# Rebuilding phi's derivative from the stored features instead of storing it: an interleaved linear-attention and sliding-window kernel, forward and backward

## The chip, the cores and the metric

The kernel runs on one core of a Trainium2 chip. The metric is the time of one execution in device microseconds; before the change the median of 3 runs is 2331.71 us (2330.03 to 2334.66). The profile shown is one further execution.

## The reference

Four layers run in turn on x of shape 2048 x 640 (32 heads of width 20), each as `x = x + block(layernorm(x))`: linear attention (A), sliding-window attention (B), A, B. The outputs are the final x and the gradients of A_x and of the four weight matrices (A's and B's are used twice each, so their gradients are summed over two layers). What matters here is block A:

```
phi = lambda t: jnp.where(t > 0, t + 1, jnp.exp(t)) + 1e-6
pq, pk = phi(q), phi(k)
kv = jnp.einsum("bhsd,bhse->bhde", pk, v)
z = jnp.einsum("bhsd->bhd", pk)
num = jnp.einsum("bhqd,bhde->bhqe", pq, kv)
den = jnp.einsum("bhqd,bhd->bhq", pq, z)[..., None] + 1e-6
o = num / den
```

The derivative of phi is min(exp(t), 1). It is also min(phi(t) - 1e-6, 1), since phi is at least 1 wherever t is positive.

## The kernel before

The 2048 rows are 16 tiles of 128 rows; a row's 640 features are handled in two chunks of 320. The run has these parts, one after the other (times from the trace):

- Forward. First the q, k, v projection of layer 0 for all tiles (to about 118 us), then passes in which layer 0's output, layer 1's window attention and layer 2's projection are interleaved by tile, then layer 3's (to about 780 us). `a_qkv` makes pq and pk: ScalarE writes `e = exp(t)` (L456), VectorE cuts it to min(e, 1) (L457) and adds max(t, 1e-6) to it (L460). Per tile SP stores pq (160 KB), e for q and k together (320 KB) and kv, that is pk beside v (320 KB), for the backward.
- Backward. `bwd_phase` and `B_attn_bwd` take turns. The linear-attention layers 2 and 0 are done in the two later calls of `bwd_phase` ("wide"). Each wide call first runs `tail` for the layer above and `lin_dO`; then `lin_grads` makes dq, dk and dv of the linear layer, tile by tile, together with `tail` of the same layer and, in the call for layer 2 only, `turn_g` and `local_dO` for the layer below. These two stretches are called the **first gradient stage** (layer 2, about 1388 to 1511 us) and the **last gradient stage** (layer 0, about 2164 to 2266 us).

Inside `forward` and `bwd_phase` nothing is ordered by hand: each operation is given to `Sched` with an engine, an assumed duration and the buffers it reads and writes. `Sched` lays all of them out with its assumed durations, lowest priority number first among those that are ready, and emits each engine's instructions in the order so found. On the chip every engine then goes through its own fixed order, and an instruction whose input is late holds everything behind it on that engine. SP issues most DMAs, among them the DMA transposes ("flips").

Names used below, per tile of a gradient stage, with the line and the engine:

- `q0 q1 k0 k1`: VectorE multiplies a chunk of dphi(q) or dphi(k) in PSUM by the derivative, `ee`, into dqkv (L1184). v0, v1 are copied by ScalarE (L1180).
- the flip `dqT<-dqkv` (L837, SP) turns the q and k part of dqkv once k1 is written; a TensorE turn and a VectorE copy (L866) do the rest. They feed 30 matmuls with wq (L843).
- `dh`: ScalarE takes the two chunks of their result (L991). Then VectorE forms three sums (L999 to L1005, the last called `sm`), ScalarE `w` (L1006), GpSimd `gw` (L1009, 128x640 f32), VectorE `gcar` (L1011), which is the running gradient.
- only in the first gradient stage: a turn of gcar with the copy `gT` (L866), matmuls with WoB, two VectorE evacuations `slab a` and `slab b` (L1052), GpSimd `prod` (L1059), VectorE `dd` (L1062) and two small operations (L1064, L1066), and the store `dOpt<-slab`, issued by ScalarE.
- loads per tile on SP: dNT and kvT (flips), `ee` (320 KB, ring of 2 buffers), hn (160 KB), and in the first gradient stage o.

In the steady part of the first gradient stage VectorE's order is gcar, q0, dd with its two small ones, q1, gT, L999 to L1005, dqT copy, k0, slab a, k1, slab b, and again gcar. ScalarE's is dh of chunk 0, the store of dOpt, dh of chunk 1, w, v0, v1. GpSimd alternates gw and prod. In the last gradient stage VectorE's order is gcar, q0, q1, L999 to L1005, dqT copy, k0, k1.

Of the kernel before, what the change touches and what calls it, by code (L numbers as in the profile page):

```python
# [11 lines left out]
ALU = mybir.AluOpType  # L12
AX = mybir.AxisListType
BF = mybir.dt.bfloat16
F32 = mybir.dt.float32
I32 = mybir.dt.int32
P = 128
# [15 lines left out]
def dve_ns(n):  # L33
    return 150 + 1.04 * n
# [139 lines left out]
class Kern:  # L174
    def __init__(self, ctx, tc, x0, A_wqkv, A_wo, B_wqkv, B_wo, grad_out, outs):
# [5 lines left out]
        D, T = self.D, self.T  # L181
# [62 lines left out]
        self.sv = {}  # L244
        for l in (0, 2):
            self.sv[l] = dict(
                pq=d.tile([T, D], BF, name=f"pq{l}"), e=d.tile([T, 2 * D], BF, name=f"e{l}"),
                kv=d.tile([T, 2 * D], BF, name=f"kv{l}"), o=d.tile([T, D], BF, name=f"o{l}"),
                r32=d.tile([T, self.H], F32, name=f"r32{l}"),
                mbd=d.tile([D, D + P], BF, name=f"mbd{l}"),  # L250
            )
# [53 lines left out]
    def forward(self):  # L305
# [7 lines left out]
        with ExitStack() as st:  # L313
# [44 lines left out]
            def dma(eng, out, in_, size, r, w):  # L358
                def f():
                    with nc.allow_non_contiguous_dma(reason="strided layouts"):  # L360
                        dq[eng].dma_start(out=out(), in_=in_())
                op(eng, 60, f, r, w, dma=("D", size))
# [71 lines left out]
            def a_qkv(l, tt, hnT):  # L434
                sv = self.sv[l]
                e, p_ = R["ee"].buf(), R["pp"].buf()

                def chunk(ci):
                    def f():
                        c0 = ci * CW  # L440
                        ps = R["half" if l == 0 and ci in (0, 2) else "mm"].buf()
                        mm_chunk(ps, CW, [(lambda k=k: hnT.t[:, k, :], lambda k=k: wsb["Wqkv_A"][:, k, c0:c0 + CW],
                                           k == 0, k == DT - 1) for k in range(DT)], [hnT, ("Wqkv_A", ci)])
                        if ci >= 4:
                            o = c0 - 2 * D
                            if ci == 4:
                                op("ACT", av(CW), lambda: nc.scalar.copy(vv[:, tt, o:o + CW], ps.t[:, 0:CW]), [ps],
                                   [("vv", tt, ci)])
                            else:
                                op("DVE", vp(CW), lambda: nc.vector.tensor_copy(vv[:, tt, o:o + CW], ps.t[:, 0:CW]),  # L450
                                   [ps], [("vv", tt, ci)])
                                dma("SP", lambda: self.tm_view(sv["kv"])[:, tt, :], lambda: kv[:, tt, :], 320 * KB,
                                    [("pk", tt, 2), ("pk", tt, 3), ("vv", tt, 4), ("vv", tt, 5)], [])
                            return
                        es = lambda: e.t[:, c0:c0 + CW]
                        op("ACT", av(CW), lambda: nc.scalar.activation(es(), ps.t[:, 0:CW], ACT.Exp), [ps], [(e, ci)])  # L456
                        op("DVE", v4(CW), lambda: nc.vector.tensor_scalar(  # L457
                            out=es(), in0=es(), scalar1=1.0, scalar2=None, op0=ALU.min), [], [(e, ci)])
                        pd = (lambda: p_.t[:, c0:c0 + CW]) if ci < 2 else (lambda: pk[:, tt, c0 - D:c0 - D + CW])
                        op("DVE", vp(CW), lambda: nc.vector.scalar_tensor_tensor(  # L460
                            out=pd(), in0=ps.t[:, 0:CW], scalar=1e-6, in1=es(), op0=ALU.max,
                            op1=ALU.add), [ps, (e, ci)], [(p_, ci) if ci < 2 else ("pk", tt, ci)])
                        if ci == 3 and l == 0 or ci == 1 and l != 0:
                            turn("half" if l == 0 else None, lambda: pqT[:, :, tt * P:(tt + 1) * P], lambda: p_.t[:, 0:D], DT,
                                 [(p_, 0), (p_, 1)], [("pqT", tt)])
                            dma("SP", lambda: self.tm_view(sv["pq"])[:, tt, :], lambda: p_.t[:, 0:D], 160 * KB,
                                [(p_, 0), (p_, 1)], [])
                        if ci == 3:
                            dma("SP", lambda: self.tm_view(sv["e"])[:, tt, :], lambda: e.t, 320 * KB,
                                [(e, i) for i in range(4)], [])  # L470
                    return f
                return [chunk(ci) for ci in range(6)]

# [328 lines left out]
    def bwd_phase(self, lb, la, nb, ahead=()):  # L802
# [8 lines left out]
        with ExitStack() as st:  # L811
# [18 lines left out]
            def dma(eng, out, in_, size, r, w):  # L830
                def f():
                    with nc.allow_non_contiguous_dma(reason="strided layouts"):
                        dq[eng].dma_start(out=out(), in_=in_())
                op(eng, 60, f, r, w, dma=("D", size))
# [59 lines left out]
            if wide:  # L894
                for name, n, shape, dt in (
                        ("dh", 1, [P, D], F32), ("w", 1, [P, D], F32), ("gw", 1, [P, D], F32), ("sm", 3, [P, 8], F32),
                        ("scr", 1, [P, D], BF), ("pq", 2, [P, D], BF), ("dNT", 2, [P, DT + 1, P], BF),
                        ("kvT", 2, [P, 2 * DT, P], BF), ("ee", 2, [P, 2 * D], BF)):
                    R[name] = ring(name, n, shape, dt)
            if not wide:  # L900
                R["om"] = ring("om", 2, [P, TT, P])
# [14 lines left out]
            def load(name, src, tt):  # L916
                b = R[name].buf()
                dma("SP", lambda: b.t, lambda: self.tm_view(src)[:, tt, :], 256 * src.shape[-1], [], [b])
                return b
# [227 lines left out]
            def lin_grads(tt, items, t0):  # L1147
                c = {}
                sv = self.sv[la]
                row = slice(tt * P, (tt + 1) * P)  # L1150

                def start():
                    for nm, src, size in (("dNT", self.tmp_dN, 192 * KB), ("kvT", sv["kv"], 320 * KB)):
                        c[nm] = b = R[nm].buf()
                        flip(lambda b=b: b.t, lambda src=src: src[row, :], size,
                             [("dNd", tt)] if nm == "dNT" else [], [b])
                    c["ee"] = load("ee", sv["e"], tt)

                def chunk(kind, ci):
                    def f():  # L1160
                        ps = R["mm"].buf()
                        e0 = ci * CW
                        ks = [k for k in range(DT) if not (self.band[k][1] <= e0 or self.band[k][0] >= e0 + CW)]
                        src, k0, rhs, key, col = {"q": ("dNT", 0, mbdT, "mbdT", 0), "k": ("kvT", DT, dmbdT, "dmbdT", D),
                                                  "v": ("kvT", 0, dmbd, "dmbd", 2 * D)}[kind]
                        b = c[src]

                        def right(k, x0, x1):
                            return lambda: rhs[:, k, e0 + x0:e0 + x1]
                        mm = [((lambda k=k: b.t[:, k0 + k, :]), right(k, x0, x1), x0, x1)  # L1170
                              for k in ks for x0, x1 in [(max(self.band[k][0] - e0, 0), min(self.band[k][1] - e0, CW))]]
                        if kind == "v":
                            mm[0] = (mm[0][0], right(ks[0], 0, CW), 0, CW)
                        else:
                            mm = [((lambda: onesx) if kind == "k" else (lambda: b.t[:, DT, :]), right(DT, 0, CW), 0, CW)] + mm
                        keys = ["mbdT"] if kind == "q" else [(key, m) for m in range(DT)]
                        banded(ps, mm, [b] + keys)
                        dst = lambda: dqkv[:, tt, col + e0:col + e0 + CW]
                        if kind == "v":
                            op("ACT", act_ns(CW), lambda: nc.scalar.copy(dst(), ps.t[:, 0:CW]), [ps],  # L1180
                               [("dqkv", tt, "v")])
                        else:
                            e, x0 = c["ee"], (D if kind == "k" else 0) + e0
                            op("DVE", dve_ns(CW), lambda: nc.vector.tensor_mul(dst(), ps.t[:, 0:CW], e.t[:, x0:x0 + CW]),  # L1184
                               [ps, e], [("dqkv", tt, kind)])
                    return f
                items.append((t0 - 0.6, start))
                for i, (kind, ci) in enumerate((k, ci) for k in "qkv" for ci in range(2)):
                    items.append((t0 + 0.15 * i, chunk(kind, ci)))
# [337 lines left out]
```

## Time and profile before

| what | value |
|---|---|
| median of 3 runs | 2331.71 us |
| the profiled execution | 2343.73 us, its span 2342.0 us, mean granted clock 0.953 |
| TensorE busy | 2051.8 us, 88% of the span |
| VectorE busy | 1470.7 us, 63% |
| ScalarE busy | 1216.0 us, 52% |
| GpSimd busy | 850.0 us, 36% |
| stores of e, 320 KB each | 32, median 2.6 us from issue to landing |
| loads of ee, 320 KB each | 32, median 3.6 us |

The span is what the profiled execution's instructions cover. The profiled execution took 12.0 us more than the median of the timed runs, so differences are worked out inside the profile and then put on the median. A row of a timeline gives the start, the time taken, engine, line, operation, what is written from what, and in brackets how long the engine sat idle before it and what it was waiting for. Instructions of one engine overlap a little: a VectorE row of 0.48 us is often followed by the next start 0.40 us later.

### The profile page before, as it was taken

What the parts mean: (1) busy time and instruction counts of PE and PEld (TensorE: products, weight loads), DVE (VectorE), ACT (ScalarE), POOL (GpSimd) and SP (SyncE); (2) the same over time, 40 slices, a digit from 0 to 9 for tenths busy, and PEclk for the clock granted to TensorE, in tenths of its full rate; (3) what the DMA queues carried; (4) which work ended last, traced back from release to release, by engine and by line L of the source; (5) the groups of instructions that cost most, each with busy time, mean ns of one, the idle gap of its engine ahead of it and who ended that gap; (6) DMA issues with size and microseconds to landing.
All of it is one profiled execution on the core that took longest, in us unless ns stands there. A gap on an engine that the chain in (4) does not pass through costs nothing. (4 is left out here: it accounts for less than half of the span.)

```text
span 2342.0 us, 68320 instructions
## 1 busy us (share of the span) xinstructions
PE 2051.8 (88%) x28146; PEld 1425.0 (61%) x28146; DVE 1470.7 (63%) x3120; ACT 1216.0 (52%) x1837; POOL 850.0 (36%) x1851
## 2 busy tenths in 40 slices
PE   6879998788888689898889979997989898998999
PEld 4556565455555457777756657754777775665664
DVE  6657776556564488999943328812889994443552
ACT  4527777527787148888822213312888882220330
POOL 1015454315656245555512203301555552221120
PEclk9989999879998799999999989997999999998999
DMA  7658999746675766667787779836766677887983
GB/s 257 199 140 191 206 195 210 175 121 163 150 162 119 204 157 133 123 136 125 143 178 168 161 185 202 171 95 147 129 126 134 126 128 161 193 181 182 208 170 100
DMA packets 921705, 377.86 MB, mean 161 GB/s; under 512 B 814000, under 2 KB 893488, under 8 KB 921136
## 3 DMA queue, kind: packets, MB, share of 16 engines
q1 hardware_dynamic: 885088, 339.82, 67.4%
q10 hardware_dynamic: 36304, 33.67, 4.4%
q8 instruction: 220, 3.60, 0.7%
q14 instruction: 93, 0.76, 0.1%
HBM read 115.34 MB, written 114.95 MB: 98 GB/s over the span
## 5 line engine op out<-in xcount | busy, mean ns | idle before, releaser
L1345 ACT ACTIVATE e_sb<-pair 128x768 bf16<-128x768 f32 x480 | 389.2, 812 | 122.6 <-PE pair L1325 115.5
L1360 DVE TENSOR_TENSOR ds_sb<-pair,e_sb 128x768 bf16<-128x768 f32 x480 | 436.0, 947 | 18.2 <-PE pair L1325 13.8
L620 ACT ACTIVATE e_sb<-s_ps 128x1536 bf16<-128x1536 f32 (+2 forms) x256 | 350.8, 1370 | 94.3 <-PE s_ps L615 46.4
L624 POOL TENSOR_SCALAR_AFFINE_SELECT e_sb<-e_sb 128x256 bf16<-128x256 bf16 x512 | 216.3, 446 | 462.7 <-ACT e_sb L620 452.9
L843 PEld LDWEIGHTS <-om 128*128 128x128 bf16 x1920 | 192.5, 101 | 179.0 <-DMA om<-o 18.6
L843 PE MATMUL mm_ps<-wq,dqT 128*128 128x320 bf16 x1920 | 284.6, 303 | 12.4 <-DMA dqT<-dqkv 12.3
L1352 POOL TENSOR_SCALAR_AFFINE_SELECT e_sb<-e_sb 128x256 bf16<-128x256 bf16 x448 | 182.5, 407 | 269.2 <-ACT e_sb L1345 260.6
L843 PE MATMUL mm_ps<-dqkv,om 128*128 128x480 bf16 x1280 | 272.3, 371 | 0.0
L1009 POOL TENSOR_TENSOR gw<-w,gcar 128x640 f32<-128x640 f32 x64 | 89.5, 1398 | 469.2 <-ACT w L1006 454.1
L843 PEld LDWEIGHTS <-dqT 128*128 128x128 bf16 x1920 | 186.8, 99 | 88.3 <-DMA dqT<-dqkv 13.8
L1349 POOL TENSOR_SCALAR_AFFINE_SELECT e_sb<-e_sb 128x256 bf16<-128x256 bf16 x512 | 207.1, 408 | 77.7 <-ACT e_sb L1345 76.3
L1389 PE MATMUL dqvk_ps<-Ksl,dsT 128*128 128x32 bf16 x2880 | 223.1, 177 | 3.0 <-DVE dqkv L1398 3.0
L991 ACT ACTIVATE dh<-mm_ps 128x320 f32<-128x320 f32 x128 | 56.0, 438 | 319.4 <-PE mm_ps L843 269.4
L1393 PE MATMUL dqvk_ps<-Qsl,ds_sb 128*128 128x32 bf16 x2880 | 220.2, 176 | 0.0
L1393 PE MATMUL dqvk_ps<-dOsl,e_sb 128*128 128x32 bf16 x2880 | 220.1, 176 | 0.0
L1373 PE MATMUL dsT_ps<-ident,ds_sb 128*128 128x128 bf16 x2244 | 192.2, 223 | 29.0 <-ACT dsT L1377 25.1
L1325 PE MATMUL pair<-KTg,QTg 32*128 32x384 bf16 (+2 forms) x1024 | 163.7, 324 | 41.6 <-DVE ds_sb L1360 32.8
L1377 ACT COPY dsT<-dsT_ps 128x768 bf16<-128x768 bf16 x240 | 190.9, 796 | 11.9 <-PE dsT_ps L1373 5.8
L1373 PEld LDWEIGHTS <-ds_sb 128*128 128x128 bf16 x2244 | 139.6, 99 | 92.1 <-issue 88.6
L393 PE MATMUL mm_ps<-Wqkv_B,hnTB 128*128 128x320 bf16 x960 | 186.2, 310 | 10.5 <-DMA hnTB<-hnB 9.0
L649 PEld LDWEIGHTS <-e_sb 128*128 128x128 bf16 x2880 | 131.5, 97 | 79.1 <-DVE e_sb L629 18.1
L1325 PE MATMUL pair<-VTg,dOTg 32*128 32x384 bf16 (+2 forms) x1024 | 163.8, 326 | 13.6 <-DMA dOTg<-dOpt 7.0
(151 smaller groups left out, 3717.1 us busy)
## 6 DMA issues: line engine op xcount, KB each, us to landing
qkvp<-qk_slab SPq DMA_DIRECT2D x32, 512.0 KB, 3.0
e<-ee SPq DMA_DIRECT2D x32, 320.0 KB, 2.6
kv<-kv SPq DMA_DIRECT2D x32, 320.0 KB, 2.7
o<-o SPq DMA_DIRECT2D x64, 160.0 KB, 3.1
om<-o SPq DMA_DIRECT2D x20, 512.0 KB, 4.5
hn<-hn SPq DMA_DIRECT2D x64, 160.0 KB, 3.1
om<-hn SPq DMA_DIRECT2D x20, 512.0 KB, 4.7
ee<-e SPq DMA_DIRECT2D x32, 320.0 KB, 3.6
```

Source lines behind the costliest of these rows:

```text
L393: nc.tensor.matmul(ps.t[:, w0:w0 + width], lhsT=lhsT(), rhs=rhs(), start=start, stop=stop)
L620: op("ACT", av(4 * nkt * P), lambda: nc.scalar.activation(e.t[:, :, 0:nkt, :], s.t[:, :, 0:nkt * P].rearrange("p h (i q) -> p h i q", q=P) ...
L624: op("POOL", 440, lambda p_=p_: nc.gpsimd.affine_select(out=e.t[:, 2 * p_:2 * p_ + 2, nkt - 1, :], in_=e.t[:, 2 * p_:2 * p_ + 2, nkt - 1, ...
L843: nc.tensor.matmul(ps.t[:, w0:w0 + width], lhsT=lhsT(), rhs=rhs(), start=start, stop=stop)
L1325: nc.tensor.matmul(ps[:, i, c0:c0 + len(ks) * P], lhsT=ld[g][lhs][r, q * P:(q + 1) * P], rhs=ld[g][rhs][r, ks[0] * P:(ks[-1] + 1) * P], st ...
L1345: nc.scalar.activation(e, PR[h][:, :, 0:3 * P].rearrange("p i (j q) -> p i j q", q=P), ACT.Exp, scale=self.c_att)
L1349: nc.gpsimd.affine_select(out=e[:, :, j, :], in_=e[:, :, j, :], compare_op=ALU.is_ge, fill=0.0, base=0, pattern=[[0, 2], [-1, P]], channel ...
L1360: nc.vector.tensor_mul(DS[n][:, hs], PR.pop(h)[:, :, 0:3 * P].rearrange("p i (j q) -> p i j q", q=P), E[n][:, hs])
L1373: nc.tensor.transpose(ps[:, i, j, :], DS[n][:, 2 * p + i, j, :], self.ident)
L1377: (nc.vector.tensor_copy if h % 2 else nc.scalar.copy)(TSB[h], TPS.pop(h))
L1389: nc.tensor.matmul(a[:, 0, hh, :], lhsT=TSB[2 * n + hh // 2][:, hh % 2, j, :], rhs=ld[g]["K"][:, k, cs], start=(i == 0), stop=(i == len(dq ...
L1393: nc.tensor.matmul(a[:, 1 + x, hh, :], lhsT=src[n][:, hh, j, :], rhs=ld[g][rhs][:, q, cs], start=(i == 0), stop=(i == len(dkv) - 1))
```

## The change

The forward no longer stores e. `ee` in the backward now has two halves: the load of the stored pq goes into one, that of the stored pk (the first half of kv's rows) into the other, 160 KB each. VectorE then turns each half in place into the derivative with one tensor_scalar (subtract 1e-6, then min with 1). These two operations per tile, 64 in all, are called `ts1` and `ts2`. The four multiplications read the halves as before.

```diff
-                pq=d.tile([T, D], BF, name=f"pq{l}"), e=d.tile([T, 2 * D], BF, name=f"e{l}"),
+                pq=d.tile([T, D], BF, name=f"pq{l}"),
...
-                        if ci == 3:
-                            dma("SP", lambda: self.tm_view(sv["e"])[:, tt, :], lambda: e.t, 320 * KB,
-                                [(e, i) for i in range(4)], [])
...
-                        ("kvT", 2, [P, 2 * DT, P], BF), ("ee", 2, [P, 2 * D], BF)):
+                        ("kvT", 2, [P, 2 * DT, P], BF), ("ee", 2, [P, 2, D], BF)):
...
-                    c["ee"] = load("ee", sv["e"], tt)
+                    c["ee"] = R["ee"].buf()
+                    for i, src in enumerate((sv["pq"], sv["kv"][:, 0:D])):
+                        dma("SP", lambda i=i: c["ee"].t[:, i, :], lambda src=src: self.tm_view(src)[:, tt, :], 160 * KB,
+                            [], [(c["ee"], i)])
+                        op("DVE", 300, lambda i=i: nc.vector.tensor_scalar(
+                            out=c["ee"].t[:, i, :], in0=c["ee"].t[:, i, :], scalar1=1e-6, scalar2=1.0,
+                            op0=ALU.subtract, op1=ALU.min), [], [(c["ee"], i)])
...
-                            e, x0 = c["ee"], (D if kind == "k" else 0) + e0
-                            op("DVE", dve_ns(CW), lambda: nc.vector.tensor_mul(dst(), ps.t[:, 0:CW], e.t[:, x0:x0 + CW]),
-                               [ps, e], [("dqkv", tt, kind)])
+                            e, i = c["ee"], int(kind == "k")
+                            op("DVE", dve_ns(CW), lambda: nc.vector.tensor_mul(dst(), ps.t[:, 0:CW], e.t[:, i, e0:e0 + CW]),
+                               [ps, (e, i)], [("dqkv", tt, kind)])
```

`Sched` lays the changed program out anew. As built, these orders differ:

- First gradient stage, VectorE, in 12 tiles of the steady part: gcar, **k1, slab b, q0**, dd with its two, q1, gT, L999 to L1005, dqT copy, k0, slab a, **ts1, ts2**, gcar. So k1 and slab b stand behind gcar instead of ahead of it. ScalarE's order there becomes dh, dh, store of dOpt, w, v0, v1. TensorE's and GpSimd's orders are the same as before.
- Last gradient stage, VectorE, in 13 tiles: ..., dqT copy, k0, **ts1, ts2**, k1, gcar, .... The ts pair of tile t+2 stands ahead of k1 of tile t+1.
- SP in the last gradient stage: ..., kvT, flip dqT of tile t (waits for k1 of tile t), hn, the two loads of tile t+2, dNT, kvT, flip dqT of tile t+1, .... In the first gradient stage the order is kvT, hn, flip dqT, the two loads, o, dNT.
- Forward: the compute engines' orders differ in the layer-0 projection only and stay the same in the interleaved passes. SP's has no stores of e, and the flips that prepare the transposed weights for the backward move into other gaps.
- SP issues as many DMAs as before (32 stores fewer, 32 loads more).

## The prediction

> **What bounds the kernel now.** I began with the busy times of the page: TensorE is busy for 88% of the span. The chain of waits only tells of the last tenth of the run, so I read the busy times by stage next, for the stages that the change touches: a slice of the first gradient stage and one of the last.
>
> ```profile
> 1450.00:1475.00 25.00, 24.52 (x234) 18.64 (x232) 22.84 (x51) 7.84 (x21) 8.10 (x6) 1.00 1.07 212
> ```
> ```profile
> 2225.00:2250.00 25.00, 23.71 (x224) 18.05 (x222) 15.90 (x40) 9.94 (x26) 5.60 (x4) 1.00 1.12 218
> ```
>
> Columns: stage, its length, busy PE, PEld, VectorE, ScalarE, GpSimd, granted clock, DMA share, GB/s. In the first gradient stage TensorE is busy for 98% but VectorE for 91% too; in the last one VectorE has a third free. DMA is full in both. So what VectorE gets more to do may matter. To see what sets the pace I followed one tile on VectorE, GpSimd and ScalarE (timelines):
>
> ```profile
> 1445.86 0.48 DVE L1052 TENSOR_TENSOR slab<-mm_ps,linv 128x320 bf16<-128x320 f32 x1
> 1446.69 1.95 DVE L1011 SCALAR_TENSOR_TENSOR gcar<-hn,sm,gw 128x640 bf16<-128x640 bf16 x1 [0.36 <-POOL gw L1009]
> 1448.57 0.48 DVE L1184 TENSOR_TENSOR dqkv<-mm_ps,ee 128x320 bf16<-128x320 f32 x1
> 1448.97 0.80 DVE L1062 TENSOR_REDUCE dd<-prod 128x32 f32<-128x640 f32 x1
> ...
> 1450.61 0.48 DVE L866 COPY gT<-mm_ps 128x640 bf16<-128x640 bf16 x1
> 1451.36 0.82 DVE L999 CUSTOM_DVE_ANT_0 scr<-dh,hn 128x640 bf16<-128x640 f32 x1 [0.28 <-ACT dh L991]
> ...
> 1452.31 0.62 DVE L866 COPY dqT<-mm_ps 128x896 bf16<-128x896 bf16 x1
> ```
> ```profile
> 1445.26 1.40 POOL L1009 TENSOR_TENSOR gw<-w,gcar 128x640 f32<-128x640 f32 x1 [5.47 <-ACT w L1006]
> 1446.61 1.35 POOL L1059 TENSOR_TENSOR prod<-slab,o 128x640 f32<-128x640 bf16 x1
> 1453.44 1.40 POOL L1009 TENSOR_TENSOR gw<-w,gcar 128x640 f32<-128x640 f32 x1 [5.48 <-ACT w L1006]
> ```
> ```profile
> 1450.41 0.35 ACTq L833 DMA_DIRECT2D dOpt<-slab  x1
> 1450.80 0.44 ACT L991 ACTIVATE dh<-mm_ps 128x320 f32<-128x320 f32 x1 [2.78 <-PE mm_ps L864]
> ...
> 1452.44 0.92 ACT L1006 ACTIVATE w<-dh,sm,rs 128x640 f32<-128x640 f32 x1 [1.11 <-DVE sm L1005]
> ```
>
> gcar starts at 1446.69 and the next one at 1454.88: 8.19 us, tile after tile. VectorE stands idle only twice, 0.28 and 0.36 us, and both are waits in one ring: gcar to q0 1.88, q0 0.40, dd with its two and q1 1.64, gT to L999 0.75, the sums until w 1.08, w to gw 1.00, gw to gcar 1.44; together 8.19. **This ring through VectorE, ScalarE and GpSimd sets the pace**; TensorE, with 24.52 of 25 us, follows closely. And gcar takes 1.95 us here, against 0.88 in the last gradient stage: it begins just as prod begins on GpSimd and ends 0.7 us after prod. VectorE is held while GpSimd works.
>
> **The change, part by part.**
>
> *Price of one ts.* The trace has no 128x640 tensor_scalar with constants. Nearest: L457, 128x320 bf16 in place, 0.24 us undisturbed; and L428, 128x640 bf16 with scalars read from SBUF, 0.43 at the least (median 0.44 and 0.49). So 0.24 to 0.44; I take 0.33, of which 0.25 is new on the queue (rows overlap by 0.08).
>
> *Is a ts held by GpSimd as gcar is?* From two timelines of the forward:
>
> ```profile
> 73.08 0.24 DVE L457 TENSOR_SCALAR ee<-ee 128x320 bf16<-128x320 bf16 x1
> 220.42 0.39 DVE L457 TENSOR_SCALAR ee<-ee 128x320 bf16<-128x320 bf16 x1 [0.21 <-ACT ee L456]
> ```
> ```profile
> 220.31 0.40 POOL L632 TENSOR_SCALAR_AFFINE_SELECT e_sb<-e_sb 128x256 bf16<-128x256 bf16 x1
> ```
>
> The same operation takes 0.24 with GpSimd idle and 0.39 where it starts 0.1 us into a GpSimd operation; it ends at 220.81, 0.10 after GpSimd does. So yes. The Trainium skill (GPSIMD Engine Reference, Specifications) has this as a rule that speaks against the change: GpSimd's SBUF interfaces are shared with VectorE, with contention for VectorE instructions in a 2-port perf mode or with two SBUF inputs. The rows agree. By the rule the ts wait for gw as worked out below; without it the time would be rival 1's.
>
> *First gradient stage.* The new order changes the ring. gcar no longer meets prod, because prod needs slab b and slab b now stands behind gcar; gcar takes 0.81 from start to start (2228.65 to 2229.46). But dd now waits for prod: the end of the slab to dd is 1.50 where nothing else delays it (dNx ends at 1208.50, dd starts at 1210.00). gT is followed by L999 without the 0.28 idle, since dh no longer queues behind the store: 0.48. New ring: gcar 0.81, k1 0.40, slab b 0.48, prod 1.50, to gT 1.64, gT 0.48, sums 1.08, w 1.00, gw 1.44 = 8.83, +0.64 a tile. Now the ts: they come 0.95 + 0.54 + 0.39 + 0.40 = 2.28 after L999 starts, while gw runs from 2.08 to 3.48 after it. So ts1 is held to gw's end and gcar waits for the rest of ts1 (0.1 to 0.36) and for ts2 (0.16 to 0.36); I take 0.45 together. Eleven rings with ts and one that begins with the reordered part but has no ts at its end: 11 x 1.09 + 0.64 = **+12.6 us**; bounds 12 x 0.64 = 7.7 and 12 x 1.36 = 16. TensorE waits for gcar's turn, so this is on the path. The loads do not add to it: their flip can start 1.3 after gcar, they land by about 6.5, the ts slot is 7.6 after gcar.
>
> *Last gradient stage.* Before, the 13 periods from gcar at 2184.64 to 2267.71 average 6.39 us; TensorE's work is 6.1, and it waits for flips:
>
> ```profile
> PE mm_ps L843 <- DMA dqT<-dqkv: 7.5, 5, 5.1
> ```
> ```profile
> 2222.84 1.25 SPq L837 DMA_TRANSPOSE dqT<-dqkv  x1
> 2224.14 1.07 SPq L833 DMA_DIRECT2D ee<-e  x1
> ```
>
> (Wait: total us, times, longest; then SP's queue.) The change adds a ring here. k1 of tile t releases the flip; then SP issues hn and both loads of tile t+2; their landing releases ts1 and ts2; and behind them on VectorE stands k1 of tile t+1, and gcar and q0 behind that. Length: flip 1.30, hn 0.49, first load 0.49, landing of the second 3.7 from its issue (160 KB hn loads in this stage: 2.5 to 5.4), ts2 0.3, k1 0.5 = 6.8. Against 6.39 that is +0.4 in 13 tiles: **+5 us**; 0 where loads land in 3.3 or less, +14 at 4.4.
>
> *Starts of the two wide calls.* Four ts of tiles 0 and 1 stand early in VectorE's queue. VectorE idles there for 9.6 us before L999 at 1201.59 and 4.0 before 1975.98, and the loads are issued 7 us and more ahead. One more issue of 0.5 on SP ahead of the next flip: +0.5, 0 to 2.
>
> *Forward.* 32 stores of 320 KB go, with 0.32 to 0.38 us of SP each; no operation of VectorE goes, since min(e, 1) is still needed. In the layer-0 projection VectorE and ScalarE wait for each other and for TensorE, never for this store, so only the new order acts: 0, between -3 and 3. In the passes from 125 to 445 us, DMA is 0.84 to 0.95 busy and TensorE waits for flips, for hnTB most:
>
> ```profile
> PE mm_ps L393 <- DMA hnTB<-hnB: 8.7, 7, 2.7
> ```
>
> With 5.8, 1.5 and 1.1 for oTA, hnTA and KT that is 17 us. The stores are 320 KB of about 3.8 MB a tile (201 GB/s for the 19 us that a tile takes), 8%, and SP fills the gap with weight flips earlier. I take -2, between -17 and +3.
>
> **Sum**: 12.6 + 5 + 0.5 - 2 = +16 us. On the profiled execution that is 2343.7 + 16 = 2360; on the median 2331.7 + 16 = **2348 us**.
>
> **The rivals.**
>
> 1. *The ts are hidden*: they slip in beside gw, and loads land fast enough in the last stage. For it: VectorE is idle for 0.36 and 1.20 ahead of gcar. Against: 220.42 above. The reorder alone is left: 7.7 + 0 + 0.5 - 2 = +6, 2338 us. Chance 0.18.
> 2. *The load ring of the last stage is longer*: landings of 4.4 and more, since DMA share is 1.12 there and VectorE now waits on every load at the head of its queue. 12.6 + 14 + 0.5 - 2 = +25, 2357 us; with landings of 5 more. Chance 0.15.
> 3. *TensorE's pace covers it*: planned order or not, the engines slide and only TensorE's work counts. Then +0 to 3 less 2: 2332. For: 98% busy. Against: a ring that sums to 8.19 exactly. Chance 0.08.
> 4. *Faster*: the stores are what makes the forward's flips late; without them the 17 us of TensorE waits go, and the back stages lose only what rival 1 says: -17 + 8 = -9, 2323 us. It decides from the point where more than 8 us of these waits go. For: DMA at 0.95. Against: 8% of the bytes, and weight flips move in. Chance 0.09.
> 5. The forecast: 0.50. That the change does not do what it says is excluded by the built order: the stores are gone, 64 ts are there.
>
> **Numbers.** Predicted 2348 us. The range takes in rivals 1 to 3 and the larger landings of rival 2, and leaves out most of rival 4: 2331 to 2365. A change of 0.2% (4.7 us) is about what the measurement of this kernel can tell from none. Slower by more: the forecast, rival 2 and most of rival 1, 0.81; within: rest of rival 1, rival 3, 0.10; faster: rival 4, 0.09.
>
> **What will show it.** First gradient stage: gcar to gcar 9.3 us instead of 8.19, gcar itself 0.88, an idle time of about 1 us ahead of dd put down to prod, ts1 longer than ts2 and ending just after gw. At 8.8 the ts were not held; at 8.2 rival 3 holds. Last stage: 6.8 instead of 6.39, with VectorE idle before a ts until its load lands; at 7.5 rival 2. Forward: the end of the interleaved passes 2 us earlier; 10 or more would be rival 4. The prediction is wrong if the reordered ring is not the one that sets the pace, or if the loads land much later than hn's do now.

## The result

| | median | range | runs |
|---|---|---|---|
| before, on the same chip | 2333.85 us | 2330.03 to 2334.66 | 5 |
| after | 2345.29 us | 2342.24 to 2348.75 | 5 |

The ratio is 1.0049, 95% interval 1.0036 to 1.0062: 11.4 us slower. The forecast was 2348 us, 16 us slower. Sign and size were as forecast, and so was the mechanism in the two gradient stages; the step for the forward was not. Three terms of the sum were off and their errors partly cancelled, so that the total came as near as it did is in part luck. The profiled execution of after took 2346.32 us (span 2344.6), 1 us over its median; that of before lay 10 us over this median. So whole spans cannot be compared here, and even milestones within them wander: the last hnB (L428) of the forward lay 7.5 us apart in the profiles of after and e1_no_ts, which have the same forward. Only periods inside one stage repeat well, and they are what is compared below.

### The profile page after: what moved, and what is told of

Same layout as the page of the kernel before. It is cut to its first block, busy times and chain, and to the rows that moved or that the text cites. A ratio compares the mean times of both kernels' runs of the same rounds, so it can differ in the third digit from the quotient of the medians.

```text
span 2344.6 us, 68343 instructions
## 1 busy us (share of the span) xinstructions
PE 2043.4 (87%) x28146; PEld 1421.6 (61%) x28146; DVE 1494.2 (64%) x3184; ACT 1217.5 (52%) x1837; POOL 852.5 (36%) x1851
## 5 line engine op out<-in xcount | busy, mean ns | idle before, releaser
L1363 DVE TENSOR_TENSOR ds_sb<-pair,e_sb 128x768 bf16<-128x768 f32 x480 | 436.3, 948 | 17.3 <-PE pair L1328 12.8
L646 PE MATMUL pv_ps<-v_slab,e_sb 128*128 128x32 bf16 x2880 | 155.1, 179 | 24.5 <-DVE oB L654 7.5
```

Source lines behind the costliest of these rows:

```text
L646: nc.tensor.matmul(pv.t[:, h % 16, :], lhsT=e.t[:, hh, j, :], rhs=vts[j].t[:, h, :], start=(j == 0), stop=(j == nkt - 1))
L1363: nc.vector.tensor_mul(DS[n][:, hs], PR.pop(h)[:, :, 0:3 * P].rearrange("p i (j q) -> p i j q", q=P), E[n][:, hs])
```

## The profile after

The two slices by stage that the prediction began with (length, busy PE, PEld, VectorE, ScalarE, GpSimd, granted clock, DMA share, GB/s):

```profile
1450.00:1475.00 25.00, 21.69 (x206) 16.52 (x205) 22.02 (x51) 7.61 (x19) 7.40 (x6) 1.00 0.85 191
2225.00:2250.00 25.00, 22.41 (x209) 16.89 (x208) 19.05 (x46) 9.94 (x26) 5.75 (x4) 1.00 0.92 198
```

At the same granted clock TensorE fell from 24.52 and 23.71 us to 21.69 and 22.41 of 25: in both stages it gets its input later. In the first gradient stage VectorE lost busy time too (22.84 to 22.02), though it was given more to do: it waits more than before. The timelines of VectorE and then GpSimd for one turn of that stage show where (after's line numbers are before's less 3; ts is L1158):

```profile
1436.78 1.61 DVE L1158 TENSOR_SCALAR ee<-ee 128x640 bf16<-128x640 bf16 x2
1438.32 0.88 DVE L1008 SCALAR_TENSOR_TENSOR gcar<-hn,sm,gw 128x640 bf16<-128x640 bf16 x1
1441.50 0.82 DVE L1059 TENSOR_REDUCE dd<-prod 128x32 f32<-128x640 f32 x1 [1.11 <-POOL prod L1056]
...
1447.37 0.87 DVE L1008 SCALAR_TENSOR_TENSOR gcar<-hn,sm,gw 128x640 bf16<-128x640 bf16 x1
```
```profile
1436.58 1.40 POOL L1006 TENSOR_TENSOR gw<-w,gcar 128x640 f32<-128x640 f32 x1 [4.16 <-ACT w L1003]
1440.13 1.34 POOL L1056 TENSOR_TENSOR prod<-slab,o 128x640 f32<-128x640 bf16 x1 [2.15 <-issue]
```

gcar to gcar is 9.05 us, where it was 8.19. Three things that the prediction named are to be seen: gcar takes 0.88 and not 1.95, because prod now runs after it; dd waits 1.11 us for prod; and the two ts, which take 0.55 us together where GpSimd is idle, take 1.61 us, because they start 0.20 after gw does. gw ends at 1437.98, and gcar starts 0.34 later. Taken singly, the first ts took 1.38 and ended 0.18 after gw; the second (0.31) started 0.10 after gw's end.

In the last gradient stage VectorE waits for loads at the head of its queue (us in total, times, longest; 2176 to 2268 us):

```profile
DVE ee L1158 <- DMA ee<-pq: 9.6, 9, 2.4
DVE ee L1158 <- DMA ee<-kv: 2.0, 4, 0.8
```

One turn of it, on VectorE, SP and GpSimd:

```profile
2242.26 0.48 DVE L1187 TENSOR_TENSOR dqkv<-mm_ps,ee 128x320 bf16<-128x320 f32 x1
...
2247.59 0.33 DVE L1158 TENSOR_SCALAR ee<-ee 128x640 bf16<-128x640 bf16 x1
2248.27 1.08 DVE L1158 TENSOR_SCALAR ee<-ee 128x640 bf16<-128x640 bf16 x1 [0.35 <-DMA ee<-kv]
2249.28 0.48 DVE L1187 TENSOR_TENSOR dqkv<-mm_ps,ee 128x320 bf16<-128x320 f32 x1
```
```profile
2242.76 1.23 SPq L834 DMA_TRANSPOSE dqT<-dqkv  x1
2244.09 0.85 SPq L830 DMA_DIRECT2D hn<-hn  x1
2244.99 0.44 SPq L830 DMA_DIRECT2D ee<-pq  x1
2245.48 0.43 SPq L830 DMA_DIRECT2D ee<-kv  x1
```
```profile
2247.62 1.55 POOL L1006 TENSOR_TENSOR gw<-w,gcar 128x640 f32<-128x640 f32 x1 [5.70 <-ACT w L1003]
```

k1 at 2242.26 releases the flip 0.50 later, then 1.33 to hn, 0.90 to the first load, 0.49 to the second, 2.79 to ts2, 1.01 to k1 of the next tile: 7.02 us, which is the load ring of the forecast. It also shows a hold that the forecast did not count here: gw begins at 2247.62, and ts2 takes 1.08 us in place of 0.33. (gw is held too: it began 0.03 after ts1 and took 1.55 in place of 1.40.) In 9 of the stage's 13 pairs one ts is held so, for 0.74 us or more. The 13 periods average 7.01 us (6.39 before); from the first gcar to the 16th the stage takes 105.1 us, where before took 96.7.

## The experiments

All ratios are to the kernel before, in runs on the same chip; 0.1% is 2.3 us. "Stage 1" is the steady gcar period of the first gradient stage, "last stage" the time from its first to its 16th gcar, and "flip waits" is the sum of all waits of TensorE for DMAs from 130 to 450 us. These three come from one profile each. Stage 1 repeats to 0.02 us among kernels of the same order there; the last stage varies from 94.0 to 96.7 us among those with before's backward order and operations.

| run | ratio, 95% interval | stage 1 | last stage | flip waits |
|---|---|---|---|---|
| before | 1 | 8.19 | 96.7 | 17.1 |
| after | 1.0049, 1.0036 to 1.0062 | 9.05 | 105.1 | 12.6 |
| e1_no_ts | 1.003, 1.002 to 1.004 | 8.75 | 99.3 | 13.8 |
| e2_drop_e | 0.9955, 0.9941 to 0.997 | 8.19 | 95.4 | 8.2 |
| e3_keep_e | 1.0074, 1.006 to 1.0089 | 9.05 | 104.6 | 18.0 |
| e4_fused | 0.9995, 0.9983 to 1.0006 | 8.18 | 98.2 | 16.7 |
| e5_fused_order | 0.9973, 0.9959 to 0.9987 | 8.18 | 99.0 | 11.8 |
| e6_after_order | 1.005, 1.0034 to 1.0067 | 9.05 | 105.2 | 10.4 |
| e7_ring3 | 1.0024, 1.0013 to 1.0034 | 8.66 | 101.3 | 18.6 |
| e8_store0 | 0.9967, 0.9952 to 0.9982 | 8.19 | 96.1 | 9.2 |
| e9_small_store | 0.9998, 0.9986 to 1.0009 | 8.18 | 94.0 | 16.9 |
| e10_fused_ring3 | 0.9969, 0.9956 to 0.9983 | 8.18 | 97.5 | 6.9 |
| e11_act_store | 0.996, 0.9945 to 0.9975 | 8.19 | 95.1 | 7.5 |
| e12_late_store | 0.9997, 0.9986 to 1.0009 | 8.18 | 95.0 | 14.4 |

The theory after the result: the gradient stages lose by the new order, the held ts and the waits for loads, and the forward gains a little by the stores' going. Its rivals: the ts cost nothing and only the order does; and the forward gains much more than forecast, so that the back must lose more.

### The backward: order, ts and loads

**e1_no_ts**: after without the two ts.

```diff
-                        op("DVE", 300, lambda i=i: nc.vector.tensor_scalar(
-                            out=c["ee"].t[:, i, :], in0=c["ee"].t[:, i, :], scalar1=1e-6, scalar2=1.0,
-                            op0=ALU.subtract, op1=ALU.min), [], [(c["ee"], i)])
+                        op("DVE", 300, lambda i=i: None, [], [(c["ee"], i)])
```

> The changed kernel with its 64 ts operations left out and every engine's order kept (so dq and dk are multiplied by the features instead of the derivative). Theory: in the first gradient stage the new order alone (gcar ahead of k1 and slab b, dd waiting for prod) costs most; gcar to gcar 8.7 us, not 9.05 as in the changed kernel and not 8.19 as before. In the last stage no ts stands between a load and k1, so the period goes back to about 6.3 to 6.5 from 7.0. Time: changed kernel less 12 x 0.35 and less 6, some 2335 us. Rival (only the ts's own time on VectorE costs, the order costs nothing): first stage back at 8.19, some 2328 us.

Measured: stage 1 at 8.75, the last stage 5.8 us shorter than after's, with periods of 6.55 on average. So the ts are 0.30 of the 0.86 us that a turn of stage 1 lost, and the new order is the other 0.56; gcar starts 0.03 after gw's end here, 0.34 in after. The time missed the expectation: 7 us above before, where the stages (+7.0 and +2.6) and the relief of the forward (5.8 in e3 below, known to about 5) would have left some 4. Forecasts of the whole from one profile's periods are no better than that here.

**e4_fused**: after without ts; the multiply itself cuts the feature to 1, so VectorE has as many operations as before.

```diff
-                            op("DVE", dve_ns(CW), lambda: nc.vector.tensor_mul(dst(), ps.t[:, 0:CW], e.t[:, i, e0:e0 + CW]),
-                               [ps, (e, i)], [("dqkv", tt, kind)])
+                            op("DVE", dve_ns(CW), lambda: nc.vector.scalar_tensor_tensor(
+                                out=dst(), in0=e.t[:, i, e0:e0 + CW], scalar=1.0, in1=ps.t[:, 0:CW], op0=ALU.min,
+                                op1=ALU.mult), [ps, (e, i)], [("dqkv", tt, kind)])
```

> The changed kernel without ts: the multiplication itself takes the derivative, as (min(feature, 1)) times PSUM in one scalar_tensor_tensor, 128 of them in place of 128 tensor_tensor (it leaves the 1e-6 in the factor). No VectorE instruction is added. Theory: the row L460 (scalar_tensor_tensor from PSUM, 0.49) against 0.48 says that the operation costs the same; VectorE's order goes back to that of before, gcar to gcar 8.2 and 6.4, and the forward keeps its gain: 2328 us, faster than both. Rival (the loads split in two cost in the last stage, or the operation is slower when its first input is in SBUF): 2334 us or more.

With no ts to place, `Sched` returns to before's order of the backward, and stage 1 to 8.18: the loss there is gone whole. But the time only came back to before's, not under it. The relief of the forward was missing, which led to e5.

**e7_ring3**: after with a third buffer for ee.

```diff
-                        ("kvT", 2, [P, 2 * DT, P], BF), ("ee", 2, [P, 2, D], BF)):
+                        ("kvT", 2, [P, 2 * DT, P], BF), ("ee", 3, [P, 2, D], BF)):
```

> The changed kernel with a third buffer for the loaded features, so that their loads no longer wait for k1 of the tile two before and may stand ahead of the flip on SP. Theory (load ring): in the last gradient stage the ts no longer wait for their loads, the period falls from 7.0 to 6.4 to 6.5, 7 us less than the changed kernel, ratio to before 1.002; the first stage stays at 9.05. Rival: the loads land late because the DMA engines are full there, then the period stays at 6.9 to 7.0 and the ratio at 1.005.

The ratio came out as expected, by a way that was only half expected. In the last stage the waits for these loads fell from 11.6 us to 3.4 and 11 of 13 periods to between 6.1 and 6.9; the mean is 6.70, not the 6.4 to 6.5 expected, as one took 9.56 with VectorE waiting for TensorE. DMA was busier there than in after (0.97 against 0.91, 2176 to 2268 us), so it was the loads' place in the rings that kept VectorE waiting, not a full DMA:

```profile
DVE ee L1158 <- DMA ee<-kv: 1.7, 4, 0.7
DVE ee L1158 <- DMA ee<-pq: 1.7, 2, 1.1
```

Several pairs of ts are held there for 1.67 us beside gw in periods of 6.13: where gcar waits for gw in any case, the hold costs nothing. In stage 1, against expectation, the planner laid another order: that of before, with the ts behind gcar. VectorE and GpSimd:

```profile
1443.29 1.95 DVE L1008 SCALAR_TENSOR_TENSOR gcar<-hn,sm,gw 128x640 bf16<-128x640 bf16 x1 [0.36 <-POOL gw L1006]
1445.17 0.55 DVE L1158 TENSOR_SCALAR ee<-ee 128x640 bf16<-128x640 bf16 x2
```
```profile
1443.21 1.35 POOL L1056 TENSOR_TENSOR prod<-slab,o 128x640 f32<-128x640 bf16 x1
```

This is the cleanest look at the hold: the same pair of ts takes 0.55 us with GpSimd idle and 1.61 beside gw. And it is gcar that meets prod again, with 1.95. The period is 8.19 + 0.47 (the pair's share of the queue) = 8.66.

### The forward: what a store cost

**e2_drop_e**: before with no store of e issued; its planned place is kept, so the order of every engine is before's.

```diff
-                            dma("SP", lambda: self.tm_view(sv["e"])[:, tt, :], lambda: e.t, 320 * KB,
-                                [(e, i) for i in range(4)], [])
+                            op("SP", 60, lambda: None, [(e, i) for i in range(4)], [], dma=("D", 320 * KB))
...
-                    c["ee"] = load("ee", sv["e"], tt)
+                    c["ee"] = load("ee", sv["kv"], tt)
```

> The kernel before with the 32 stores of e left out and every order kept; the backward loads rows of kv (same size and shape of rows) where it loaded e, so dq and dk are wrong by that factor. Theory: the forward gets some 2 to 4 us shorter since TensorE waits less for flips in the interleaved passes; the gradient stages stay at 8.19 and 6.4. About 2330 us. Rival (the stores are what delays the forward): 10 us or more, 2323 us or less.

Missed by far: 10.5 us less. The rival was right on this: TensorE's waits for flips in the interleaved passes (PE, 130 to 450 us) fall from 17.1 us to 8.2, mostly those for hnTB, 8.7 before:

```profile
PE mm_ps L393 <- DMA oTA<-oA: 5.3, 4, 2.3
PE mm_ps L393 <- DMA hnTB<-hnB: 2.0, 3, 1.3
```

**e3_keep_e**: after with the stores of e put back (nothing reads them).

> The changed kernel with the stores of e put back (written, never read). Theory: slower than the changed kernel by what the stores cost in the forward, 2 to 5 us: some 2349 us, with 9.05 and 7.0 in the gradient stages. Rival (the stores cost 10 us or more): 2355 us or more.

17.3 us over before. Its forward is before's, so this is the price of the backward: 10.4 us in stage 1 (from first to last gcar 131.8 us in after, whose periods it has, against 121.4 in before) and 8 in the last. Against after it is 0.25% or 5.8 us: the relief of the forward in the change. The two intervals together leave it anywhere from 1 to 10 us.

**e8_store0**: as e2, but layer 0's stores are issued (`if l == 0`).

> The kernel before with the e stores of layer 0 kept and those of layer 2 not issued (order unchanged; the backward loads rows of the k and v features in their place, so the derivative is another one). Theory: the stores cost where DMA is 0.84 to 0.95 busy, which is where layer 2's are (130 to 450 us): 8 to 10 us less than before, ratio 0.996. Rival: they cost in the layer-0 projection, where VectorE and ScalarE take turns; then 0 to 2 us less, ratio 0.999 to 1.

7.7 of e2's 10.5 us are there with layer 2's stores alone; those stand in the interleaved passes. The rest, 2.8, would be layer 0's 16 stores; the two intervals are too wide to tell it from nothing.

**e9_small_store**: the store stays where it is, with its wait, but writes 32 of 1280 columns.

```diff
-                            dma("SP", lambda: self.tm_view(sv["e"])[:, tt, :], lambda: e.t, 320 * KB,
+                            dma("SP", lambda: self.tm_view(sv["e"])[:, tt, 0:32], lambda: e.t[:, 0:32], 320 * KB,
```

> The kernel before, order unchanged, with every e store still issued on SP and waiting for e as before, but of 32 columns of 1280 (the backward loads rows of the k and v features in place of e, so the derivative is another one). It tells what of a store cost the 10.5 us of e2. Theory: the bytes, which lie on the DMA engines ahead of the flips that TensorE waits for; then nearly the whole relief is there, ratio 0.9955 to 0.997, and the waits for hnTB in 130 to 450 us are 2 to 3 us as in e2. Rival: the place in SP's queue (32 issues of 0.35 us and their waits for e hold the flips behind them); then the time is that of before, ratio 0.999 to 1.001, and the waits for hnTB stay at 5 to 9 us.

The theory of the bytes fell. DMA share in 130 to 450 us went from 0.84 to 0.82, just as in e2, and the time stayed at before's, with TensorE's waits for flips:

```profile
PE mm_ps L393 <- DMA oTA<-oA: 7.4, 7, 2.5
PE mm_ps L393 <- DMA hnTB<-hnB: 5.3, 5, 1.5
```

On SP the small store takes as long as the whole one: 0.57 to 0.58 us in 10 of its 13 rows from 130 to 450 us, against 0.53 for most of before's.

**e11_act_store** and **e12_late_store**: all bytes are written. In e11 ScalarE issues the stores; in e12 SP does, each right behind the kv store of its tile, when e has long been there.

```diff
-                            dma("SP", lambda: self.tm_view(sv["e"])[:, tt, :], lambda: e.t, 320 * KB,
-                                [(e, i) for i in range(4)], [])
+                            op("SP", 60, lambda: nc.scalar.dma_start(out=self.tm_view(sv["e"])[:, tt, :], in_=e.t),
+                               [(e, i) for i in range(4)], [], dma=("D", 320 * KB))
```

> The kernel before with all its e stores whole, issued by ScalarE's queue in place of SP's, in the same planned place; the order on the other engines is unchanged. Theory after e9 (what a store costs is its place in SP's in-order queue, not its bytes): most of e2's relief is there with the bytes still written, ratio 0.996 to 0.998; a part is lost where ScalarE waits for VectorE's min or spends 32 x 0.35 us on the issues. Rival (bytes on the DMA engines): ratio 1.000.

> The kernel before with all its e stores whole and on SP, but each issued right behind the kv store of its tile, a step later, when e has long been there (a few rows of TensorE trade places). It parts the two sides of a place in SP's queue. Theory: it is the wait for e at the head of the queue that holds the flips behind it; without it most of the relief is there, ratio 0.996 to 0.998. Rival: it is the slots themselves (32 issues of about 0.35 us on SP); ratio 0.999 to 1.001.

e11 keeps the relief as far as the intervals tell, at a DMA share of 0.87:

```profile
PE mm_ps L393 <- DMA oTA<-oA: 3.9, 5, 1.1
PE mm_ps L393 <- DMA hnTB<-hnB: 2.9, 4, 1.2
```

e12 has none of it. So neither the bytes nor the wait at the head of SP's queue was the price, but **the slot on SP**. The SP queues of before and then e2 show it:

```profile
227.53 1.23 SPq L365 DMA_TRANSPOSE QT<-qk_slab  x1
228.87 0.53 SPq L361 DMA_DIRECT2D e<-ee  x1
229.44 1.24 SPq L365 DMA_TRANSPOSE wT<-Wo_B  x1
230.78 1.23 SPq L365 DMA_TRANSPOSE hnTB<-hnB  x1
```
```profile
228.70 1.23 SPq L365 DMA_TRANSPOSE QT<-qk_slab  x1
230.03 1.23 SPq L365 DMA_TRANSPOSE wT<-Wo_B  x1
231.31 1.27 SPq L365 DMA_TRANSPOSE hnTB<-hnB  x1
```

The queue has no gap here; the store moves the flip of hnTB, for which TensorE waits, back by 0.57 us. From QT's flip to hnTB's it is 3.25 us in before, 3.19 in e9 and 2.61 in e2; the medians of 12 tiles are 4.60, 4.62 and 3.97 (4.28 in e11). Once issued, hnTB lands as soon with the store as without (median 2.8 us in before, 2.7 in e2 and e11), so it is the issue that comes late and not the transfer. e12 moves the slot to another flip: from QT to hnTB it is 3.97 again, but 10 of the 13 stores from 130 to 450 us now stand right ahead of oTA's flip, and TensorE waits there instead:

```profile
234.58 0.44 SPq L454 DMA_DIRECT2D e<-ee  x1
235.11 1.39 SPq L365 DMA_TRANSPOSE oTA<-oA  x1
```
```profile
PE mm_ps L393 <- DMA oTA<-oA: 8.5, 6, 2.8
PE mm_ps L393 <- DMA hnTB<-hnB: 2.6, 3, 1.1
```

SP's rows fill 267 of the 320 us from 130 to 450, and 13 of layer 2's 16 stores stand there. 13 x 0.57 is 7.4 us, near the 7.7 measured for that layer (4 to 11 by its interval); SP also has 53 us free there, so the match is no proof. The Trainium skill (DMA: Bandwidth & Descriptors, Issuing engines are not separate DMA queues) says that starting DMAs on several engines only saves the sequencer's time to start them, "which is usually small relative to the DMA itself". Both halves agree with the rows: the start takes 0.53 us and the store lands 2.6 us after it (median). Small as it is, it was the price: moving 32 such starts is the whole of e11's 0.4%.

**e5_fused_order** and **e6_after_order**: e4 and after with the line of e2 in place of the store, which puts before's order of the forward back.

> The fused multiply of e4, with before's order of the forward put back: the planner is told of an e store that is not issued. Theory: the new layer-0 order gives back about 4 us of what the stores' going brings, so with the old order the relief of e2 (10.5 us) stays and the last gradient stage costs 1 to 3 of it. Ratio to before 0.996 to 0.997, some 9 us less; periods 8.2 and 6.5 as in e4. Rival: the order costs nothing and e4 lost the relief in the backward; then the ratio is e4's, 0.9995.

> The changed kernel with the same order of the forward put back and no store. Theory, as for e5: e3's +17.3 us less e2's 10.5 is +7 us, ratio 1.003, periods 9.05 and 7.0 as in after. Rival: the order costs nothing, then the ratio is that of the changed kernel, 1.005 (11 us).

e5 agrees with the theory, e6 does not: it is level with after. The flip waits fall in both pairs, by 4.9 us (16.7 to 11.8) and by 2.2 (12.6 to 10.4). Of the kernels without stores, those with the new order have 12.6 to 18.6 us of such waits and those with the old one 6.9 to 11.8; this fits weight flips standing in the stores' place on SP, but no run moves those flips alone. How much time the new order costs is not settled: 0.22% in the one pair, nothing in the other, each to about 0.2%.

**e10_fused_ring3**: e5 with a third buffer for ee.

> e5 (fused multiply, before's order of the forward, no store) with a third buffer for the loaded features. Theory: what e5 lacks to e2 (0.9973 against 0.9955, 4 us) is in part the two loads that SP issues behind dqT's flip in the last gradient stage; with the third buffer they stand elsewhere, and the period of the last stage falls from 6.5 to 6.3, 2 to 3 us less than e5, ratio 0.996. Rival: the two loads cost the same wherever they stand; ratio 0.997, period 6.5.

Faster than both kernels at 0.9969, though not to be told from e5; the periods of the last stage fell from 6.57 on average to 6.46, not to the 6.3 expected. e11, which leaves the backward alone, stands at 0.996, not to be told from these either: **what the change could gain was to be had by issuing the same store from another queue.**

## Why the prediction came out right, point by point

- *Price of one ts*, 0.33 us: right; single rows are 0.31 to 0.33.
- *A ts is held by GpSimd*: right, 1.61 us for the pair beside gw against 0.55. The Trainium skill (GPSIMD Engine Reference, Specifications) has GpSimd's SBUF interfaces as shared with VectorE, with contention for instructions in a 2-port perf mode or with two SBUF inputs; the runs agree, and the held ts1 ended 0.18 us after gw's end.
- *Reordered ring*, +0.64 a turn: measured 0.56 (e1). Its parts were right: gcar short, dd waiting for prod 1.11.
- *Hold of the ts*, +0.45: measured 0.30. gcar starts 0.34 after gw's end instead of 0.03: 0.10 until ts2 starts, at the low end of the 0.1 to 0.36 given for ts1's rest, and 0.24 from there to gcar. First stage: +10.4 in place of +12.6, inside its bounds.
- *Last gradient stage*, +5: the ring was the right one, its size was not: +8 against before's profile, which has the longest last stage of the six kernels with its order and operations, and up to +11 against the others. Term by term in the turn shown: hn 0.90 instead of 0.49, the landing 2.8 instead of 3.7, ts2 with gw's hold 1.0 instead of 0.3. The hold had been counted in the first stage alone. The waits for loads go where no ts stands behind them (e1) and mostly where the loads have a third buffer (e7). One reading was off too: of the 7.5 us that TensorE waited for dqT, 5.1 were one wait ahead of the 13 periods (2164 to 2184 us); inside them it was 2.4.
- *Starts*, +0.5: no run tells it apart.
- *Forward*, -2: this is the step that failed. In the change it is about -6 (after against e3, -1 to -10), and the stores alone were worth -10.5 (e2). The step priced them as 8% of the bytes; they cost a slot on SP each, and the slot is 0.57 us in these passes, not the 0.32 to 0.38 read from the layer-0 projection. Its remark that weight flips fill the gap fits the flip waits of the new order; that they kept the rest of the relief from arriving is not shown, since e6, with the old order, gained nothing. Rival 4's effect came in e2 (8.9 us of the waits and 10.5 us of the time went), but for another reason than its DMA at 0.95, and in the change only 4.5 us of the waits went, of the more than 8 that it asked for.

The measured terms give 10.4 + 8 - 6 = +12, or up to +15 with the other last stages, against 11.4 measured (8 to 14 by its interval); the forecast's sum was 16. The forward's term is too loosely known for this to be a test.

## What to carry to other kernels

Price a DMA that goes or comes first by the slot it takes in its issuer's queue, read in the stage where it stands and with what is queued behind it; its bytes may be worth nothing that can be measured, as in e9. When an operation is added to VectorE, look at what GpSimd runs in that place, and try first to fold it into an operation that is there anyway. And when a load is to feed an instruction earlier than before, count its buffers, since a ring that is one short makes the load follow the work it was to feed.

## What was not expected of the hardware

The same kind of store took 0.32 to 0.38 us of SP's time early in the forward and 0.53 in the interleaved passes, where it stands between flips; issued by ScalarE there, it took 0.33. And taking 10 MB of writes away left the time where it was, though 13 of the 32 stores stand where DMA was 0.84 busy (e9).
